# Two weight halves, one tile's statistics on another engine, and Newton steps tile by tile, in a sliding-attention plus gated-MLP kernel

## The chip, the cores and the metric

The kernel runs on one core of a Trainium2 chip. The metric is the device time of one execution in microseconds (us). The core has five engines that run side by side, each taking its own instructions in order: TensorE (PE in the profile, with its weight loads as PEld), VectorE (DVE), ScalarE (ACT), GpSimd (POOL) and SyncE (SP), which here only issues DMA transfers. An engine waits where an instruction needs what another engine or a transfer has not delivered yet.

## The reference

`x` is 2048 tokens by 512 features, in bf16. Both branches read its layernorm `xn`; their outputs are added to `x`.

```python
xn = _layernorm(x, axis=-1)                       # (x - m) / sqrt(v + 1e-5)
# branch A: 32 heads of 16, each token attends to 8 earlier tokens, 2 apart
qkv = xn @ wqkv;  logits = q . k[pos - 2*w] * 16**-0.5;  attn = softmax(logits)
A = (attn-weighted sum of v) @ wo
# branch B: gated MLP with a token-mixing matrix
z  = gelu(xn @ w_in)                              # 2048 x 1376
z1 = z[:, :688];  z2 = _layernorm(z[:, 688:])
g  = w_sp @ z2 + b_sp[:, None]                    # 2048 x 2048 mixing over tokens
B  = (z1 * g) @ w_out
out = x + A + B
```

## The kernel before

The tokens are cut into 16 tiles of 128 rows. The order of the instructions on every engine is written out by hand (`tc.manual_schedule()`): an engine executes what the program issues to it in program order, and semaphores between engines follow from the data. TensorE carries nearly all of the span, in this order: `z2` for tiles 0 to 3, the q and k products, further `z2` tiles between them, head sums (`reduce_heads`), v products, the token mixing (`mix`), the `z1` tiles, and the two output products.

The change is in the first 30 us, which prepare `xn` and start TensorE:

- **Loads.** SP issues, in order, rows of tile 0 and tile 1 (L169, L170), the rows of tiles 2 and 3 together (L171), all 688 columns of the `z2` weights `w_z2` (L172, in the profile `w_z`), then the further rows (`load_x`, L165) and the q and k weights `wqk`. The bias `b_sp` is loaded on ScalarE's queue as 16 rows of 128 (L91), turned by TensorE (L351) and copied by ScalarE into `b_col`.
- **Layernorm of tiles 0 to 3.** `ln_stats(i)` is a `bn_stats` and a `bn_aggr` on VectorE (L185, L186); `roots` is a square root on ScalarE (L194); `recip` a reciprocal on VectorE (L348); `ln_apply` writes the normalised tile `xn` on VectorE (L190); `transpose_pe` turns it in four 128x128 pieces on TensorE (L212) and copies it into `xnT`, on ScalarE for tiles 0 and 1 (L214) and on VectorE for tiles 2 and 3 (L216).
- **Spins.** `spin(n)` issues n small matmuls on a tile of ones (L100) whose results nobody reads; they keep TensorE busy before there is data.
- **`z2` tiles.** One tile is 8 matmuls of 344 columns, 4 slices `kc` of the inner dimension by 2 column halves `hh` (L229), into a pair of PSUM banks (three pairs take turns); ScalarE then applies gelu (L234). Tiles 0 to 3 run as soon as `xnT` has them, and the q and k products of tokens 0 to 511 (`qk_pair`, L272) follow.
- **Layernorm of tiles 4 to 15.** This goes in groups of two tiles. Per group VectorE computes the statistics and three small integer and float steps that give a first guess of 1/sqrt (L200 to L202); GpSimd refines both tiles' guesses by two Newton steps, four small operations each (L204 to L207); VectorE applies, and SP issues a transposing DMA per tile into `xnT` (L219). The loop issues for each round: statistics of group g, guess and Newton steps of group g, then apply and transposes of the group before.

After tile 15's apply VectorE starts `products(0, 0)` and `products(0, 1)` (L301), whose sums `reduce_heads(0, 0)` and `reduce_heads(0, 1)` take on TensorE (L310).

Of the kernel before, what the change touches and what calls it, by code (L numbers as in the profile page):

```python
# [7 lines left out]
BF16 = mybir.dt.bfloat16  # L8
F32 = mybir.dt.float32
ACT = mybir.ActivationFunctionType  # L10
ALU = mybir.AluOpType
PSUM = bass.MemoryType.PSUM

P = 128
S = 2048
D = 512
NT = S // P
C = D // P
H = 32
DH = 16  # L20
DHA = 14
W = 8
DIL = 2
HALO = 16
# [4 lines left out]
F = 1376  # L29
FH = 688  # L30
FHALF = 344
# [10 lines left out]
NEWTON_C = (1.19462228, 1.5 / 1.407904506 ** 2)  # L42
# [3 lines left out]
def kernel(  # L46
# [16 lines left out]
    V = nc.vector  # L63
    A = nc.scalar
    G = nc.gpsimd
    PE = nc.tensor
    SP = nc.sync
# [6 lines left out]
    const = ctx.enter_context(tc.tile_pool(name="const", bufs=1))  # L74
# [7 lines left out]
    ps_aux = pair_b.enter_context(tc.tile_pool(name="ps_aux", bufs=2, space=PSUM))  # L82
    turn = [0]

    def bank_pair(name, two=False):
        turn[0] += 1
        pool = ps_b if turn[0] % 3 == 0 and not two else ps_a
        return pool.tile([P, 2, 512], F32, name=name, tag="mm")

    b16 = const.tile([NT, P], BF16, name="b16")  # L90
    A.dma_start(b16[:], B_b_sp.rearrange("(j p) -> j p", p=P))  # L91


    ones = const.tile([P, P], BF16, name="ones")
    V.memset(ones[:], 1.0)
# [2 lines left out]
    def spin(n):  # L98
        for _ in range(n):
            PE.matmul(idle[:, 0, 0:P], ones[:], ones[:], start=True, stop=True)  # L100

    spin(26)

    ident = const.tile([P, P], BF16, name="ident")
    G.memset(ident[:], 0.0)
# [4 lines left out]
    for c in range(C):  # L110
# [3 lines left out]
                        base=15 - 128 * c, pattern=[[16, 32]], channel_multiplier=-1)  # L114
    mask = const.tile([32, W, HALO], F32, name="mask")
    G.memset(mask[:], 0.0)
    G.affine_select(out=mask[:], in_=mask[:], compare_op=ALU.is_ge, fill=NEG,
                    base=-DIL * (W - 1), pattern=[[DIL, W], [1, HALO]], channel_multiplier=0)
    b_col = const.tile([P, NT], F32, name="b_col")
    stats = const.tile([P, NT, 6], F32, name="stats")  # L120
    mv = const.tile([P, NT, 2], F32, name="mv")
    rstd = const.tile([P, NT], F32, name="rstd")
    hv = const.tile([P, NT], F32, name="hv")
    nt = const.tile([P, NT], F32, name="nt")
    eps_t = const.tile([P, 1], F32, name="eps_t")
# [5 lines left out]
    zrstd = const.tile([P, NT], F32, name="zrstd")  # L131
# [8 lines left out]
    xnT = rpool.tile([P, C, S], BF16, name="xnT")  # L140
# [11 lines left out]
    xnp = early.enter_context(tc.tile_pool(name="xnp", bufs=6))  # L152
    w_z2 = e1.tile([P, C, FH], BF16, name="w_z2")
    wqk = e1.tile([P, C, 2, D], BF16, name="wqk")
    junk = e1.tile([P, FH], BF16, name="junk")


    w_in_r = B_w_in.rearrange("(k p) f -> p k f", p=P)
    wqkv_r = A_wqkv.rearrange("(k p) f -> p k f", p=P)
    xq = []  # L160
# [7 lines left out]
    x0 = xqp.tile([P, 4, D], BF16, name="xq")  # L168
    SP.dma_start(x0[:, 0, :], x2[0:P, :])  # L169
    SP.dma_start(x0[:, 1, :], x2[P:2 * P, :])  # L170
    SP.dma_start(x0[:, 2:4, :], x2[2 * P:4 * P, :].rearrange("(i p) d -> p i d", p=P))  # L171
    SP.dma_start(w_z2[:], w_in_r[:, :, FH:F])  # L172
    xq.append(x0)
    load_x(1)
    for s in range(2):
# [7 lines left out]
    def ln_stats(i):  # L183
        xs = xq[i // 4][:, i % 4, :]
        V.bn_stats(stats[:, i, :], xs)  # L185
        V.bn_aggr(mv[:, i, :], stats[:, i, :])  # L186

    def ln_apply(i):
        xn = xnp.tile([P, D], BF16, name="xn")
        V.tensor_scalar(xn[:], xq[i // 4][:, i % 4, :], mv[:, i, 0:1], rstd[:, i:i + 1], ALU.subtract, ALU.mult)  # L190
        return xn

    def roots(a, b):
        A.activation(rstd[:, a:b], mv[:, a:b, 1], ACT.Sqrt, bias=eps_t[:])  # L194

    def ln_newton(a, b):

        sl = slice(a, b)
        y, h, t = rstd[:, sl], hv[:, sl], nt[:, sl]
        V.tensor_scalar(h, mv[:, sl, 1], EPS, -0.5 / NEWTON_K, ALU.add, ALU.mult)  # L200
        V.tensor_scalar(t.bitcast(I32), h.bitcast(I32), 1, 0x3FFFFFFF, ALU.logical_shift_right, ALU.bitwise_and)
        V.tensor_scalar(y.bitcast(I32), t.bitcast(I32), -1, SEED, ALU.mult, ALU.add)  # L202
        for c in NEWTON_C:
            G.tensor_tensor(t, y, y, ALU.mult)  # L204
            G.tensor_tensor(t, t, h, ALU.mult)
            G.tensor_scalar(t, t, c, None, ALU.add)
            G.tensor_tensor(y, y, t, ALU.mult)  # L207

    def transpose_pe(i, xn):
        pt = ps_aux.tile([P, C, P], BF16, name="pt", tag="aux")  # L210
        for c in range(C):
            PE.transpose(pt[:, c, :], xn[:, c * P:(c + 1) * P], ident[:])  # L212
        if i < 2:
            A.copy(xnT[:, :, i * P:(i + 1) * P], pt[:])  # L214
        else:
            V.tensor_copy(xnT[:, :, i * P:(i + 1) * P], pt[:])  # L216

# [3 lines left out]
    def z2_start(i):  # L221
        pz = bank_pair("pzb")
        for kc in range(C):
            z2_part(i, pz, kc)
        return pz

    def z2_part(i, pz, kc):
        for hh in range(2):
            PE.matmul(pz[:, hh, 0:FHALF], xnT[:, kc, i * P:(i + 1) * P],  # L229
                      w_z2[:, kc, hh * FHALF:(hh + 1) * FHALF],  # L230
                      start=(kc == 0), stop=(kc == C - 1))

    def z2_gelu(i, pz):
        A.activation(z2[:, i, :].rearrange("p (a b) -> p a b", a=2), pz[:, :, 0:FHALF],  # L234
                     ACT.Gelu_apprx_tanh, accum_out=zsum[:, i:i + 1])
# [4 lines left out]
    def z2_tile(i):  # L240
        z2_gelu(i, z2_start(i))
# [13 lines left out]
    def qk_chunk(b, c):  # L255
        tsl = slice(b * 512, (b + 1) * 512)
        pq = bank_pair("pq")
        for s in range(2):
            for kc in range(C):
                PE.matmul(pq[:, s, :], wqk[:, kc, s, c * P:(c + 1) * P], xnT[:, kc, tsl],  # L260
                          start=(kc == 0), stop=(kc == C - 1))
        at = HALO + b % 2 * 512
        A.copy(qk[b // 2][:, :, c, at:at + 512], pq[:])  # L263
# [83 lines left out]
    def recip(i):  # L347
        V.reciprocal(rstd[:, i:i + 1], rstd[:, i:i + 1])  # L348

    pb = ps_aux.tile([P, NT], BF16, name="pb", tag="aux")  # L350
    PE.transpose(pb[:], b16[:], ident[0:NT, 0:NT])  # L351
    spin(9)
    ln_stats(0)
    roots(0, 1)
    A.copy(b_col[:], pb[:])
    ln_stats(1)
    roots(1, 2)
    recip(0)
    transpose_pe(0, ln_apply(0))
    recip(1)  # L360
    spin(4)
    transpose_pe(1, ln_apply(1))
    spin(4)
    ln_stats(2)
    roots(2, 3)
    ln_stats(3)
    roots(3, 4)
    pz0 = z2_start(0)
    z2_gelu(0, pz0)
    recip(2)  # L370
    xn2 = ln_apply(2)
    recip(3)
    xn3 = ln_apply(3)
    pz1 = bank_pair("pzb")
    for kc in range(2):
        z2_part(1, pz1, kc)
    transpose_pe(2, xn2)
    for kc in range(2, C):
        z2_part(1, pz1, kc)
    transpose_pe(3, xn3)  # L380
    z2_gelu(1, pz1)
    z2_tile(2)
    z2_tile(3)


# [2 lines left out]
    for g in groups + (None,):  # L388
        if g:
            for i in range(*g):  # L390
                ln_stats(i)
            ln_newton(*g)
        if prev:
            for i in range(*prev):
                transpose_dma(i, ln_apply(i))
            if prev[0] == 6:
                SP.dma_start(wv[:], wqkv_r[:, :, 2 * D:3 * D])
        prev = g


# [14 lines left out]
    qk_chunk(1, 2)  # L415
    z2_square(5)
    qk_chunk(1, 3)
    for j in range(5):
        load_wsp(j)
        if j == 1:  # L420
            SP.dma_start(w_z1[:], w_in_r[:, :, 0:FH])
# [116 lines left out]
    op = late2.tile([P, DH, NB * TG], BF16, name="op")  # L538
    wo_r = late2.tile([P, DHA, D], BF16, name="wo_r")
    wout = late2.tile([P, MCH, D], BF16, name="wout")  # L540
    G.memset(wout[32:64, MCH - 1, :], 0.0)

    def op_rest(hb, q):

        for k in range(NG):
            for e in range(2):
                q.dma_start(uT[64 + 32 * e:96 + 32 * e, MCH - 1, hb * SB + k * TG:hb * SB + (k + 1) * TG],
                             op[32 * k:32 * k + 32, DHA + e, hb * TG:(hb + 1) * TG])

# [41 lines left out]
    for j in range(3, NT):  # L591
# [6 lines left out]
        if j == 5:  # L598
            SP.dma_start(wout[:, 0:MCH - 1, :], B_w_out[0:(MCH - 1) * P, :].rearrange("(m p) n -> p m n", p=P))
            SP.dma_start(wout[0:FTAIL, MCH - 1, :], B_w_out[(MCH - 1) * P:FH, :])  # L600
            for e in range(2):
                SP.dma_start(wout[64 + 32 * e:96 + 32 * e, MCH - 1, :],
                             A_wo.rearrange("(h d) n -> d h n", d=DH)[DHA + e])
        if 6 <= j < 10:
            k = j - 6
            SP.dma_start(wo_r[32 * k:32 * k + 32, :, :], A_wo.rearrange("(h d) n -> h d n", d=DH)[:, 0:DHA, :])
        if 11 <= j < 13:
# [34 lines left out]
    def out_a(jj, first):  # L642
        for k in range(NG):
            if first:
                pos[jj, k] = ps_o[jj % 2].tile([P, D], F32, name="po")
        for d in range(DHA):
            for k in range(NG):
                PE.matmul(pos[jj, k][:], op[32 * k:32 * k + 32, d, jj * P:(jj + 1) * P],  # L648
                          wo_r[32 * k:32 * k + 32, d, :], start=first and d == 0,
                          stop=(not first or (jj, k) == (3, NG - 1)) and d == DHA - 1, tile_position=(32 * k, 0))  # L650

# [54 lines left out]
```

## Time and profile before

| | |
|---|---|
| time, median of 3 runs | 206.74 us (206.56 to 206.85) |
| the profiled execution: time, span | 206.28 us, 204.6 us |
| TensorE busy | 199.7 us, 98% of the span |
| VectorE, ScalarE, GpSimd busy | 81%, 46%, 8% |
| granted TensorE clock | 1.0 of full speed |
| first `z2` matmul starts | 6.73 us |
| first q/k matmul (`qk_pair`) starts | 11.84 us |
| last apply (tiles 14, 15) starts | 28.68 us |
| `products(0, 0)` and `(0, 1)`, together | 30.49 to 39.24 us |
| first `reduce_heads` matmul | 41.94 us |

The profiled execution is 1.68 us longer than its span: launch and end lie outside of it. Times inside the profile count from the start of the span. The chain of waits is followed back from the last instruction, each step to what released it; a line of it with a queue's name and "q" is the issuing of a transfer. Starts of pipelined instructions can lie a little before the end of the one ahead.

### The profile page before, as it was taken

What the parts mean: (1) busy time and instruction counts of PE and PEld (TensorE: products, weight loads), DVE (VectorE), ACT (ScalarE), POOL (GpSimd) and SP (SyncE); (2) the same over time, 40 slices, a digit from 0 to 9 for tenths busy, and PEclk for the clock granted to TensorE, in tenths of its full rate; (3) what the DMA queues carried; (4) which work ended last, traced back from release to release, by engine and by line L of the source; (5) the groups of instructions that cost most, each with busy time, mean ns of one, the idle gap of its engine ahead of it and who ended that gap; (6) DMA issues with size and microseconds to landing.
All of it is one profiled execution on the core that took longest, in us unless ns stands there. A gap on an engine that the chain in (4) does not pass through costs nothing.

```text
span 204.6 us, 4062 instructions
## 1 busy us (share of the span) xinstructions
PE 199.7 (98%) x1666; PEld 120.1 (59%) x1666; DVE 165.9 (81%) x192; ACT 93.6 (46%) x145; POOL 16.1 (8%) x82
## 2 busy tenths in 40 slices
PE   7999999999999999999999999999999999999994
PEld 6655544555566666656666666666666664444442
DVE  4799949659299499989999999999999988335263
ACT  3868897676879996335733331223333311000000
POOL 5045640000000000100000000000000000000000
PEclk9999999999999999999999999999999999999999
DMA  6974957999000004707857799999756225015633
GB/s 167 365 225 79 187 107 153 187 215 145 0 3 0 3 0 41 170 20 161 125 119 153 176 201 187 196 165 205 141 144 141 56 48 80 10 41 153 240 109 96
DMA packets 67395, 25.64 MB, mean 125 GB/s; under 512 B 57152, under 2 KB 67248, under 8 KB 67248
## 3 DMA queue, kind: packets, MB, share of 16 engines
q1 hardware_dynamic: 66960, 25.24, 58.2%
q8 instruction: 13, 0.21, 0.5%
q10 hardware_dynamic: 416, 0.14, 0.3%
q14 instruction: 6, 0.05, 0.1%
HBM read 9.79 MB, written 2.10 MB: 58 GB/s over the span
## 4 chain that ended last, share of the span: by engine, by line
PE 95%; DMA 2%; SPq 1%; DVE 0%; issue 0%
PE pg L492 37%; PE pq L260 10%; PE po L639 10%; PE pzb L229 9%; PE pz L504 9%; PE pv L285 7%; PE po L648 6%; PE pl L310 4%; PE pq L272 3%; DMA w_z<-in_B_w_in_dram 2%; PE po L621 1%; PE pt L212 0%; SPq L171 0%; DVE ot L623 0%; SPq L170 0%; SPq L169 0%
## 5 line engine op out<-in xcount | busy, mean ns | idle before, releaser
L492 PE MATMUL pg<-z,wspT 128*128 128x344 bf16 x512 | 77.3, 309 | 0.0
L492 PEld LDWEIGHTS <-wspT 128*128 128x128 bf16 x512 | 50.0, 98 | 24.9 <-issue 0.4
L301 DVE TENSOR_TENSOR pr<-qk 128x8192 bf16<-128x8192 bf16 x8 | 35.0, 4424 | 7.4 <-PE pl L310 7.4
L495 ACT ACTIVATE gs<-pg,b_col 128x688 bf16<-128x688 f32 x16 | 13.4, 835 | 52.8 <-PE pg L492 52.8
L558 DVE TENSOR_TENSOR pw<-vp,a_sb 128x4096 bf16<-128x4096 bf16 x16 | 36.2, 2286 | 0.0
L260 PE MATMUL pq<-xnT,wqk 128*128 128x512 bf16 x96 | 21.5, 379 | 0.0
L504 PE MATMUL pz<-w_z,xnT 128*128 128x344 bf16 x128 | 21.3, 309 | 0.0
L229 PE MATMUL pzb<-w_z,xnT 128*128 128x344 bf16 x128 | 20.1, 309 | 0.3 <-DMA w_z<-in_B_w_in_dram 0.3
L639 PE MATMUL po<-wout,uT 128*128 128x512 bf16 x90 | 19.8, 379 | 0.0
L563 DVE TENSOR_TENSOR pw<-pw 128x4096 bf16<-128x4096 bf16 x8 | 18.3, 2289 | 0.1
L655 DVE TENSOR_TENSOR ot<-po,xr 128x512 bf16<-128x512 f32 x15 | 9.7, 687 | 9.4 <-PE po L648 6.9
L229 PEld LDWEIGHTS <-xnT 128*128 128x128 bf16 x128 | 12.3, 98 | 7.2 <-issue 0.7
L504 PEld LDWEIGHTS <-xnT 128*128 128x128 bf16 x128 | 12.4, 98 | 6.5 <-issue 0.4
L260 PEld LDWEIGHTS <-wqk 128*128 128x128 bf16 x96 | 9.3, 98 | 10.9 <-issue 0.4
L639 PEld LDWEIGHTS <-uT 128*128 128x128 bf16 x90 | 8.7, 98 | 10.7 <-issue 0.4
L263 ACT CAST qk<-pq 128x1024 bf16<-128x1024 f32 x12 | 12.2, 1013 | 5.4 <-PE pq L260 5.4
L285 PE MATMUL pv<-xnT,wv 128*32 128x512 bf16 x256 | 14.6, 380 | 0.0
L509 ACT ACTIVATE z<-pz 128x688 bf16<-128x688 f32 x16 | 11.9, 745 | 5.6 <-PE pz L504 5.2
L238 ACT ACTIVATE junk<-z 128x688 bf16<-128x688 bf16 x16 | 12.5, 779 | 0.2
L234 ACT ACTIVATE z<-pzb 128x688 bf16<-128x688 f32 x16 | 11.8, 737 | 1.4 <-PE pzb L229 1.4
L648 PE MATMUL po<-wo_r,op 32*128 32x512 bf16 x224 | 12.3, 374 | 0.0
L285 PEld LDWEIGHTS <-wv 128*32 128x32 bf16 x256 | 9.4, 139 | 4.6 <-issue 0.3
(81 smaller groups left out, 167.5 us busy)
## 6 DMA issues: line engine op xcount, KB each, us to landing
xr<-in_A_x_dram SPq DMA_DIRECT2D x4, 512.0 KB, 4.2
out_dram<-ot SPq DMA_DIRECT2D x15, 128.0 KB, 1.8
wo_r<-in_A_wo_dram SPq DMA_DIRECT2D x4, 448.0 KB, 5.0
w_z<-in_B_w_in_dram SPq DMA_DIRECT2D x2, 688.0 KB, 4.9
xq<-in_A_x_dram SPq DMA_DIRECT2D x2, 512.0 KB, 7.0
wqk<-in_A_wqkv_dram SPq DMA_DIRECT2D x2, 512.0 KB, 7.1
wout<-in_B_w_out_dram SPq DMA_DIRECT2D x1, 640.0 KB, 5.0
a_sb<-in_A_x_dram SPq DMA_DIRECT2D x1, 512.0 KB, 9.2
```

The source lines that it names most:

```text
L229: PE.matmul(pz[:, hh, 0:FHALF], xnT[:, kc, i * P:(i + 1) * P], w_z2[:, kc, hh * FHALF:(hh + 1) * FHALF], start=(kc == 0), stop=(kc == C - 1))
L238: A.activation(junk[:], z2[:, i, :], ACT.Square, accum_out=zsq[:, i:i + 1])
L260: PE.matmul(pq[:, s, :], wqk[:, kc, s, c * P:(c + 1) * P], xnT[:, kc, tsl], start=(kc == 0), stop=(kc == C - 1))
L285: PE.matmul(pv[32 * k:32 * k + 32, dd, :].rearrange("p (b t) -> p b t", b=NB), wv_v[:, kc, 2 * d2 + dd, :], xnT_g[:, kc, :, k, :], start=( ...
L301: V.tensor_tensor(pr[:], qk[hb][:, 0, :, HALO:HALO + SB].unsqueeze(1).broadcast_to([P, 2, C, SB]), shifted(qk[hb][:, 1, :, off:off + SB]), ...
L492: PE.matmul(pg[:, hh, 0:FHALF], wsps[j][:, k, :], z2[:, k, hh * FHALF:(hh + 1) * FHALF], start=(k == 0), stop=(k == NT - 1))
L495: A.activation(gs[:], pg[:, :, 0:FHALF], ACT.Identity, bias=b_col[:, j:j + 1])
L504: PE.matmul(pz[:, hh, 0:FHALF], xnT[:, kc, j * P:(j + 1) * P], w_z1[:, kc, hh * FHALF:(hh + 1) * FHALF], start=(kc == 0), stop=(kc == C - 1))
L558: V.tensor_tensor(pw[:], shifted(vp[:, :, hb, off:off + P]), a_sb[:, 2 * p:2 * p + 2, osl].unsqueeze(2).broadcast_to([P, 2, DH, P]), ALU.mult)
L563: V.tensor_tensor(pws[p - 1][:], pws[p - 1][:], pw[:], ALU.add)
L639: PE.matmul(pos[jj, k][:], uT[:, m, i * P:(i + 1) * P], wout[:, m, :], start=first and m == 0, stop=not first and m == MCH - 1)
L648: PE.matmul(pos[jj, k][:], op[32 * k:32 * k + 32, d, jj * P:(jj + 1) * P], wo_r[32 * k:32 * k + 32, d, :], start=first and d == 0, stop=(n ...
```

## The change

The first rows are unchanged, but `w_z2` is loaded in two transfers, columns 0 to 343 ahead of the rows of tiles 2 and 3 and columns 344 to 687 behind them. Tiles 0 and 1 take the first column half first: the order on TensorE is transposes 0, spin(7), transposes 1, then (tile 0, half 0), (tile 1, half 0), (tile 0, half 1), transposes 2, (tile 1, half 1), half of tile 2, transposes 3, the rest of tile 2, tile 3. The copies of `xnT` on ScalarE are cut in two.

Tile 1's mean and variance come from ScalarE: an Identity with a running sum, a Square with a running sum, and a square root. A first square root on a constant stands ahead of everything on ScalarE. Tile 4's `bn_stats` goes in two halves into the start-up of tiles 2 and 3.

The Newton steps run per tile in two fused operations instead of four, so a group still has eight, each one column wide with one or two of its scalars read per partition from memory. In the loop, the guess and the Newton steps of group g now come behind apply and transposes of the group before.

The bias is loaded by a transposing DMA on SP's queue after tile 15's transposes, and copied by GpSimd. The 26 + 9 spins become one run of 35.

```diff
-    b16 = const.tile([NT, P], BF16, name="b16")
-    A.dma_start(b16[:], B_b_sp.rearrange("(j p) -> j p", p=P))
-    spin(26)
+    spin(35)
...
     SP.dma_start(x0[:, 1, :], x2[P:2 * P, :])
+    SP.dma_start(w_z2[:, :, 0:FHALF], w_in_r[:, :, FH:FH + FHALF])
     SP.dma_start(x0[:, 2:4, :], x2[2 * P:4 * P, :].rearrange("(i p) d -> p i d", p=P))
-    SP.dma_start(w_z2[:], w_in_r[:, :, FH:F])
+    SP.dma_start(w_z2[:, :, FHALF:FH], w_in_r[:, :, FH + FHALF:F])
...
-        for c in NEWTON_C:
-            G.tensor_tensor(t, y, y, ALU.mult)
-            G.tensor_tensor(t, t, h, ALU.mult)
-            G.tensor_scalar(t, t, c, None, ALU.add)
-            G.tensor_tensor(y, y, t, ALU.mult)
+        for i in range(a, b):
+            y, h, t = rstd[:, i:i + 1], hv[:, i:i + 1], nt[:, i:i + 1]
+            for c in NEWTON_C:
+                G.tensor_scalar(t, y, y, h, ALU.mult, ALU.mult)
+                G.tensor_scalar(y, t, c, y, ALU.add, ALU.mult)
...
         if i < 2:
-            A.copy(xnT[:, :, i * P:(i + 1) * P], pt[:])
+            for c in range(0, C, 2):
+                A.copy(xnT[:, c:c + 2, i * P:(i + 1) * P], pt[:, c:c + 2, :])
...
+    def z2_half(i, pz, hh):
+        for kc in range(C):
+            z2_part(i, pz, kc, (hh,))
...
-    pb = ps_aux.tile([P, NT], BF16, name="pb", tag="aux")
-    PE.transpose(pb[:], b16[:], ident[0:NT, 0:NT])
-    spin(9)
+    A.activation(zrstd[:, 0:1], eps_t[:], ACT.Sqrt)
     ln_stats(0)
+    A.activation(junk[:, 0:D], x0[:, 1, :], ACT.Identity, scale=-1.0 / D, accum_out=mv[:, 1, 0:1])
     roots(0, 1)
-    A.copy(b_col[:], pb[:])
-    ln_stats(1)
-    roots(1, 2)
+    A.activation(junk[:, 0:D], x0[:, 1, :], ACT.Square, bias=mv[:, 1, 0:1], accum_out=mv[:, 1, 1:2])
+    A.activation(rstd[:, 1:2], mv[:, 1, 1:2], ACT.Sqrt, bias=eps_t[:], scale=1.0 / D)
     recip(0)
     transpose_pe(0, ln_apply(0))
+    spin(7)
     recip(1)
-    spin(4)
-    transpose_pe(1, ln_apply(1))
-    spin(4)
+    xn1 = xnp.tile([P, D], BF16, name="xn")
+    V.tensor_scalar(xn1[:], x0[:, 1, :], mv[:, 1, 0:1], rstd[:, 1:2], ALU.add, ALU.mult)
+    transpose_pe(1, xn1)
     ln_stats(2)
     roots(2, 3)
     ln_stats(3)
     roots(3, 4)
-    pz0 = z2_start(0)
+    pz0 = bank_pair("pzb")
+    pz1 = bank_pair("pzb")
+    z2_half(0, pz0, 0)
+    z2_half(1, pz1, 0)
+    z2_half(0, pz0, 1)
     z2_gelu(0, pz0)
     recip(2)
     xn2 = ln_apply(2)
     recip(3)
+    transpose_pe(2, xn2)
+    z2_half(1, pz1, 1)
+    z2_gelu(1, pz1)
     xn3 = ln_apply(3)
-    pz1 = bank_pair("pzb")
-    for kc in range(2):
-        z2_part(1, pz1, kc)
-    transpose_pe(2, xn2)
-    for kc in range(2, C):
-        z2_part(1, pz1, kc)
+    pz2 = bank_pair("pzb")
+    z2_part(2, pz2, 0)
+    z2_part(2, pz2, 1)
+    V.bn_stats(stats4[:, 0, :], xq[1][:, 0, 0:D // 2])
     transpose_pe(3, xn3)
-    z2_gelu(1, pz1)
-    z2_tile(2)
+    V.bn_stats(stats4[:, 1, :], xq[1][:, 0, D // 2:D])
+    V.bn_aggr(mv[:, 4, :], stats4[:])
+    z2_part(2, pz2, 2)
+    z2_part(2, pz2, 3)
+    z2_gelu(2, pz2)
     z2_tile(3)
...
         if g:
             for i in range(*g):
-                ln_stats(i)
-            ln_newton(*g)
+                if i > 4:
+                    ln_stats(i)
         if prev:
             for i in range(*prev):
                 transpose_dma(i, ln_apply(i))
...
+        if g:
+            ln_newton(*g)
         prev = g
...
     qk_chunk(1, 3)
+    SP.dma_start_transpose(b_t[:], B_b_sp.rearrange("(j p) -> j p", p=P))
+    G.tensor_copy(b_col[:], b_t[:])
```

More of the change, by code (lines that the diff above doesn't have):

```diff
@@ L21 @@
 DHA = 14
+ZV = (7, 8, 13, 14, 15)
 W = 8
@@ L119 @@
     b_col = const.tile([P, NT], F32, name="b_col")
+    b_t = const.tile([P, NT], BF16, name="b_t")
+    stats4 = const.tile([P, 2, 6], F32, name="stats4")
     stats = const.tile([P, NT, 6], F32, name="stats")
@@ L225, in z2_start, with z2_part @@
         return pz
-    def z2_part(i, pz, kc):
-        for hh in range(2):
+    def z2_half(i, pz, hh):
+        for kc in range(C):
+            z2_part(i, pz, kc, (hh,))
+    def z2_part(i, pz, kc, halves=(0, 1)):
+        for hh in halves:
             PE.matmul(pz[:, hh, 0:FHALF], xnT[:, kc, i * P:(i + 1) * P],
```

## The prediction

> **What bounds the kernel now.** I read the page's chain of waits first, then the same chain for the first 13 us, then the timeline of ScalarE, VectorE and GpSimd up to 45 us.
>
> ```profile
> PE 95%; DMA 2%; SPq 1%; DVE 0%; issue 0%
> ...
> 2.19 4.50 DMA w_z<-in_B_w_in_dram
> 6.69 0.04 issue
> 6.73 1.91 PE pzb L229 x12
> ```
>
> From 6.73 us on TensorE is the chain, without a gap, to the last 3 us. So only two things can count: when that stream starts, and whether the change opens a gap in it. The weights hold the start only just: by TensorE's timeline the weight load for the first `z2` matmul was at 6.35 us, and the wait for `w_z` was 0.31 us. Nothing else on TensorE moves, so the head cannot bring more than a few tenths.
>
> The rows of ScalarE and VectorE that feed tiles 0 and 1:
>
> ```profile
> 3.75 0.18 DVE L186 BATCH_NORM_AGGREGATE mv<-stats 128x2 f32<-128x6 f32 x1
> ...
> 4.64 0.13 DVE L348 RECIPROCAL rstd<-rstd 128x1 f32<-128x1 f32 x1
> 4.81 0.41 DVE L190 TENSOR_SCALAR xn<-xq,mv,rstd 128x512 bf16<-128x512 bf16 x1
> 5.13 0.16 DVE L348 RECIPROCAL rstd<-rstd 128x1 f32<-128x1 f32 x1
> ...
> 7.27 0.13 DVE L348 RECIPROCAL rstd<-rstd 128x1 f32<-128x1 f32 x1
> ```
>
> And one round of the later tiles: GpSimd's first steps of the group of tiles 6 and 7, VectorE's apply of tiles 4 and 5 beside them, the last apply, and the products behind it.
>
> ```profile
> 14.65 0.19 POOL L204 TENSOR_TENSOR nt<-rstd 128x2 f32<-128x2 f32 x1
> 14.92 0.20 POOL L205 TENSOR_TENSOR nt<-nt,hv 128x2 f32<-128x2 f32 x1
> ...
> 14.66 0.73 DVE L190 TENSOR_SCALAR xn<-xq,mv,rstd 128x512 bf16<-128x512 bf16 x2
> ...
> 28.68 0.73 DVE L190 TENSOR_SCALAR xn<-a_sb,mv,rstd 128x512 bf16<-128x512 bf16 x2 [1.79 <-POOL rstd L207]
> 30.40 0.18 DVE L424 COPY qk<-qk 128x64 bf16<-128x64 bf16 x1 [0.99 <-ACT qk L263]
> 30.49 8.75 DVE L301 TENSOR_TENSOR pr<-qk 128x8192 bf16<-128x8192 bf16 x2
> ```
>
> Today VectorE sets the pace of these rounds (applies at 14.66, 17.53, 20.39: 2.87 us each), and GpSimd's eight steps (about 0.28 us from start to start, 2.25 together) hide beside the next statistics. The products end at 39.24; the second `reduce_heads`, which needs them, starts 0.92 us (16 of 32 matmuls in 1.84) after 42.01, at 42.93. That cover of 3.7 us is what the change uses up.
>
> **The head, step by step.** Tile 1's rows land at 1.26 + 2.3 = 3.56 us (issue and landing of L170). Identity over 512 from SBUF: the Square over 688 takes 0.78; the 1024 cast against the 512 copy gives (1.013 - 0.587) / 512 = 0.83 ns an element, so 0.78 - 0.15 = 0.63 us. Its accumulator read starts 0.10 before its end and lasts 0.20, as at L238: mean at 4.31. Tile 0's root is queued behind it, at 4.22 instead of 3.96, ends 4.52; reciprocal 4.59 instead of 4.64, because VectorE has lost tile 1's statistics. So tile 0 gains 0.05 only. The Square reads a bias, which is worth 0.09 (L495 0.835 against L509 0.745): from 4.43, sum at 5.25; root 5.29 to 5.59; tile 1's reciprocal at 5.66, against 5.13 now.
>
> From that reciprocal to the transposes of tile 1 is 0.66 us (5.13 to 5.79), and 0.24 more to what follows on TensorE (6.03). The transposes of tile 1 stand ahead of the first half of `z2`, so TensorE starts at 6.56: 0.17 gained on 6.73. The first 344 columns do not hold it: tiles 2 and 3's 256 KB, issued at the same 1.72, landed 2.9 us later, so 344 KB land by about 5.3.
>
> But VectorE now runs 0.53 late. Reciprocal 1 to reciprocal 2 is 2.14 as before, to the transposes 0.66: tile 2's transposes start at 8.46. TensorE, with 12 matmuls at 0.146, is there at 8.35: 0.1 wait. Transposes 0.40, copy 0.43, three hops of about 0.035: tile 2 usable at 9.36, TensorE there at 9.26: 0.1. The same for tile 3: 10.84 against 10.74: 0.1. Eight matmuls later the q/k products start at 12.01, against 11.84. **Head: +0.17 us**, the gain eaten by three waits. Bounds: if ScalarE's chain were as quick as VectorE's (reciprocal 1 at 5.13), 6.1 us from there (2.80 to tile 2's transposes, then 20 matmuls and two transposes, 3.3) gives 11.2, -0.6; a chain 0.2 slower gives +0.4.
>
> The second half of `w_z2` is needed at 7.75. All of it landed at 6.69; the bytes ahead of it are the same, but its rows are 688 bytes, so 512 packets more. At the present 63 ns of a packet (60% of 5 us on 16 engines for 764) over 16 engines that is at most 2.0 us, at the least 0. I take 0.4, near the bytes: landing 7.1, no wait; the upper end gives 0.9.
> [...] No run here shows 688-byte rows yet.
>
> The dummy root, the split copies and tile 4's early statistics go into idle stretches. The gelu table load (1.28) moves to 8.2, gelu of tile 0 to 9.5, needed by tile 3's matmuls at 10.8. The bias leaves TensorE and ScalarE and puts one transposing DMA on SP, some 1.2 us by L219, ahead of the `w_sp` loads, which are first used at 73 us: nothing. GpSimd's copy waits for that DMA; only memsets of `z1` stand behind it.
>
> **The rounds.** Behind the change the guess for the next group waits in VectorE's queue behind the second apply, which waits for GpSimd's eighth step. So the chain closes on itself: one round is 8 steps plus about 1.0 us (0.03 to the apply, 0.33 to the next slot, three guesses of 0.21 less overlap 0.58, 0.08 to GpSimd). With g from step to step, the first group starts at 12.8, tile 15's step ends at 12.8 + 48 g + 5.0, the two products end 0.5 + 8.75 later: 27.1 + 48 g. TensorE needs them at 42.93 + 0.15 = 43.1. **The cover is gone at g = 0.333; beyond, each 10 ns costs 0.48 us.**
>
> What is g? The trace shows no GpSimd operation with scalars read from memory. Lower end: L204 to L207 as they are, 0.28. An immediate tensor_scalar, L206, steps at 0.30. Upper end by other engines' pointers: on ScalarE 0.09 each; on VectorE, L252 against L190 (0.459 for 688, 0.411 for 512) leave 0.27 fixed where L244 has 0.163, 0.054 for each of two. New operations have two and one pointers, 1.5 on average: 0.30 + 0.135 = 0.435. GpSimd's own second stream operand costs nothing (L205 0.213 with two, L206 0.217 with one). I take half of VectorE's price, 0.027 each: **g = 0.34**, between these two rows. That is 48 x 0.007 = 0.35 us at the products, and 0.1 to 0.2 at the q/k products of tokens 512 to 1023, which need tile 7: its transpose would land at 22.5 (second round's step end 19.2 + apply 0.45, + landing 2.6 with some 0.2 of queue), against 22.25 + 0.15.
> [...]
>
> **Sum.** Head +0.17, rounds +0.35 and +0.15, rest 0: +0.7 us. On the profiled execution 206.28 + 0.7 = 207.0; its 206.28 lies 0.46 under the median, to which I add the same: **207.4**.
>
> **Rivals.** (a) *GpSimd's pointers are nearly free*, g up to 0.33: the rounds grow to 3.4 to 3.65 us but stay under the 3.7 us cover; only the head remains, 206.9, no change. For it: L205 against L206. Against it: both other engines pay. (b) *Faster*: ScalarE's sums come early and tile 2 is not late; reciprocal 1 before 5.3 and g under 0.33, time 206.1 to 206.4. It needs 0.35 us off a chain whose every row is measured on other shapes. (c) *GpSimd pays in full*, g 0.37 to 0.43: tile 6, tile 11 and tile 15 come late too; products alone give +1.8 to +4.7, time 208.7 to 211.6. (d) The second weight half lands late, up to +0.9 at the head: 0.05, inside the others' ranges.
>
> **Numbers.** Forecast (g 0.333 to 0.37) 0.33; (a) with (d) 0.29; (b) 0.13; (c) 0.25. Range 206.2 to 210.5 leaves out half of (c) and part of (b). 0.2%, 0.4 us, is about what a measurement of this kernel can tell from no change. Faster 0.13, same 0.29, slower 0.58.
>
> **What would show it.** Right: the first `z2` matmul near 6.55 and q/k near 12.0; VectorE idle before the reciprocal of tile 1, released by ScalarE; GpSimd steps near 0.34; the second apply of each round waiting for GpSimd; products starting near 34.5, and TensorE waiting before its second head sum. Wrong: GpSimd steps at or below 0.30 with products before 33; q/k starting before 11.6; or a TensorE wait on the second weight half.

## The result: 2.6 us slower, nearly all of it in the closed loop of GpSimd and VectorE

| | before | changed |
|---|---|---|
| median | 206.68 us | 209.31 us (209.05 to 209.59, 4 runs) |
| ratio to before | | 1.0131 (95%: 1.0118 to 1.0145) |
| profiled execution: time, span | 206.28, 204.6 us | 209.53, 207.8 us |
| first `z2` matmul, first q/k matmul | 6.73, 11.84 us | 6.62, 12.71 us |
| GpSimd's work for two tiles, first start to last end | 2.2 us | 3.0 us |
| one round of two tiles | 2.87 us | 4.03 us |
| `products(0, 0)` and `(0, 1)` end | 39.24 us | 46.08 us |

The profiled executions lie 0.40 under the median of before and 0.22 over the median of the changed kernel, so their difference, 3.25 us, overstates the change by 0.62. Medians and ratios here leave out the few executions that ran at a lower granted clock (one of the six of run e4 below: 355.67 us at 0.56).

The page's chain of waits, changed kernel. TensorE had 95% of it before:

```profile
PE 77%; DVE 9%; POOL 7%; issue 2%; DMA 2%; SPq 1%
```

Most of the first 46 us of the chain has moved to other engines. The timelines of VectorE and GpSimd for the third round (start, duration, engine and line, operation, what ended the idle time before it):

```profile
21.33 0.17 DVE L203 TENSOR_SCALAR rstd<-nt 128x2 int32<-128x2 int32 x1
...
24.64 0.41 DVE L191 TENSOR_SCALAR xn<-xq,mv,rstd 128x512 bf16<-128x512 bf16 x1 [1.06 <-POOL rstd L208]
24.96 0.16 DVE L201 TENSOR_SCALAR hv<-mv 128x2 f32<-128x2 f32 x1
...
25.36 0.17 DVE L203 TENSOR_SCALAR rstd<-nt 128x2 int32<-128x2 int32 x1
...
36.90 0.41 DVE L191 TENSOR_SCALAR xn<-a_sb,mv,rstd 128x512 bf16<-128x512 bf16 x1 [1.06 <-POOL rstd L208]
```

```profile
21.60 0.34 POOL L207 TENSOR_SCALAR nt<-rstd,hv 128x1 f32<-128x1 f32 x1 [1.03 <-DVE rstd L203]
22.04 0.26 POOL L208 TENSOR_SCALAR rstd<-nt,rstd 128x1 f32<-128x1 f32 x1
...
24.33 0.26 POOL L208 TENSOR_SCALAR rstd<-nt,rstd 128x1 f32<-128x1 f32 x1
25.63 0.34 POOL L207 TENSOR_SCALAR nt<-rstd,hv 128x1 f32<-128x1 f32 x1 [1.03 <-DVE rstd L203]
```

Read them as one circle. VectorE's guess ends at 21.50, GpSimd works from 21.60 to 24.59, the second apply waits 1.06 us for it and starts at 24.64, the next guess stands behind that apply and ends at 25.53, and GpSimd, idle for 1.03 us, starts at 25.63. Each engine waits once for the other: 4.03 us a round. What this costs is in the timeline of TensorE, first before, then changed:

```profile
22.25 7.07 PE L260 MATMUL pq<-xnT,wqk 128*128 128x512 bf16 x32
...
30.32 7.07 PE L260 MATMUL pq<-xnT,wqk 128*128 128x512 bf16 x32
...
41.94 1.91 PE L310 MATMUL pl<-pr,rsel 128*32 128x512 bf16 x32
43.68 3.63 PE L285 MATMUL pv<-xnT,wv 128*32 128x512 bf16 x64
```

```profile
23.49 7.08 PE L266 MATMUL pq<-xnT,wqk 128*128 128x512 bf16 x32
...
31.95 7.07 PE L266 MATMUL pq<-xnT,wqk 128*128 128x512 bf16 x32 [0.21 <-DMA xnT<-xn]
...
43.57 1.05 PE L316 MATMUL pl<-pr,rsel 128*32 128x512 bf16 x16
46.12 1.05 PE L316 MATMUL pl<-pr,rsel 128*32 128x512 bf16 x16 [1.51 <-DVE pr L307]
```

The lines are the q/k products of tokens 512 to 1023, those of tokens 1024 to 1535 and the head sums; the v products behind the sums start at 43.68 before and at 46.98 now. The lag of the changed kernel is 0.87 us after the head, then 1.24, 1.63, 1.63 and, behind the second head sum, 3.30. From there to the end it stays: 1.67 of it is the wait for the products, 0.76 the transposes of tiles 6, 7 and 11 landing late.

These parts are not separate prices. From the second head sum to the end of the span both profiles take 161.7 us (204.6 - 42.93 and 207.8 - 46.12), and in the changed kernel that sum starts 0.04 us after the products end. So the end of the products alone sets the time there: without the earlier waits TensorE would have waited longer at this place. The products end 6.84 us later than before; 1.1 of that is the later first step of GpSimd (13.54 against 12.44), the rest the longer rounds, and 3.7 was cover.

The head, in VectorE's timeline:

```profile
5.41 0.16 DVE L354 RECIPROCAL rstd<-rstd 128x1 f32<-128x1 f32 x1 [0.42 <-ACT rstd L362]
5.61 0.41 DVE L368 TENSOR_SCALAR xn<-xq,mv,rstd 128x512 bf16<-128x512 bf16 x1
6.86 0.69 DVE L186 BATCH_NORM_STATS2 stats<-xq 128x6 f32<-128x512 bf16 x1 [0.84 <-DMA xq<-in_A_x_dram]
```

Tile 1's reciprocal waits for ScalarE, as expected, but then comes a wait that the prediction did not have: the rows of tiles 2 and 3, now queued behind the first weight half, land at 2.19 + 4.65 = 6.84 us.

### The profile page after: what moved, and what is told of

It reads as the page before. It is cut to its first block, busy times and chain, and to the rows that moved or that the text cites. A ratio compares the mean times of both kernels' runs of the same rounds, so it can differ in the third digit from the quotient of the medians.

```text
span 207.8 us, 4069 instructions
## 1 busy us (share of the span) xinstructions
PE 201.6 (97%) x1664; PEld 120.6 (58%) x1664; DVE 165.7 (80%) x191; ACT 95.0 (46%) x151; POOL 21.2 (10%) x83
## 4 chain that ended last, share of the span: by engine, by line
PE 77%; DVE 9%; POOL 7%; issue 2%; DMA 2%; SPq 1%
PE pg L511 36%; PE po L658 9%; PE pz L523 9%; PE pv L291 7%; PE po L667 6%; PE pzb L235 5%; DVE pr L307 4%; POOL nt L207 4%; POOL rstd L208 3%; PE pl L316 3%; DMA xq<-in_A_x_dram 2%; PE pq L266 2%; DVE xn L191 1%; DVE stats L186 1%; PE po L640 1%
## 5 line engine op out<-in xcount | busy, mean ns | idle before, releaser
L235 PE MATMUL pzb<-w_z,xnT 128*128 128x344 bf16 x128 | 20.7, 310 | 0.0
```

## The experiments

### Which part costs it: operations and place, apart and together

The GpSimd part has two edits: the operations (four for two tiles at once, against two fused ones per tile) and the place (ahead of the apply of the group before, or behind it). Three kernels undo one or both in the changed kernel, a fourth puts both into the kernel before. All four ran on one chip.

```diff
 # e1: both undone.  e2: place undone.  e3: operations undone.
-            for c in NEWTON_C:
-                G.tensor_scalar(t, y, y, h, ALU.mult, ALU.mult)
-                G.tensor_scalar(y, t, c, y, ALU.add, ALU.mult)
+        for c in NEWTON_C:                       # e1, e3
+            G.tensor_tensor(t, y, y, ALU.mult)
...
+            ln_newton(*g)                        # e1, e2: ahead of transpose_dma(i, ln_apply(i))
         if prev:
...
-        if g:
-            ln_newton(*g)
```

Both undone:

> The changed kernel with the whole GpSimd part put back: the four unfused operations for two tiles at once, issued ahead of the apply of the group before. My theory has two separate losses, the head (q/k start 0.87 us later, because VectorE waits for the rows of tiles 2 and 3 behind the first weight half) and the closed loop of GpSimd and VectorE (2.4 us). It expects the head alone: q/k at about 12.7 us, no wait of TensorE behind it, rounds of 2.9 us, time 207.1 to 207.6. Rival 1, all of the loss is the loop: 206.7. Rival 2, the head costs most: 208.5 or more.

Only the place undone:

> The changed kernel with the fused per-tile operations kept, but the guess and the Newton steps issued ahead of the apply of the group before, as in the kernel before. My theory: GpSimd's 3.0 us of a group then set the rounds by themselves (3.0 us instead of 4.03), tile 15's apply at 31.5 to 32, products end near 41, before TensorE needs them (43.8), so the time is that of the kernel with the whole GpSimd part put back, 207.1 to 207.6. Rival, the dearer operations are the loss wherever they stand: 209.0 to 209.3.

Only the operations undone:

> The changed kernel with the four unfused operations for two tiles at once, kept at the new place behind the apply. My theory: a round is 2.25 + 1.03 = 3.3 us, tile 15's apply near 32.3, products end near 41.5, TensorE needs them at 43.8: no wait, 207.1 to 207.6. Rival, the place alone is the loss: 209.0 to 209.3.

Nothing but the GpSimd part, in the kernel before:

> The kernel before with nothing but the GpSimd part of the change: fused per-tile operations behind the apply. My theory: first step at 12.4 us, rounds of 4.03, second apply of the last round at 35.7, products end at 44.9 where TensorE needs them at 42.93: 2.0 us lost, 208.7 (208.4 to 208.9). Rival, the loop only hurts because the head is already late: at most 207.2.

| kernel | median, us | ratio to before (95%) |
|---|---|---|
| before, same runs | 206.59 | |
| both undone (e1) | 206.64 | 0.9998 (0.9981 to 1.0016) |
| place undone, fused operations (e2) | 207.03 | 1.002 (1.0001 to 1.004) |
| operations undone, new place (e3) | 206.97 | 1.0012 (0.9995 to 1.0029) |
| before with both (e4) | 208.57 | 1.0096 (1.0062 to 1.013) |

Either edit alone costs 0.4 us (the intervals reach 0.8 and 0.6); both together cost 2.0, in a kernel whose head is untouched. So place and price act together, as the closed loop has it. VectorE's timeline for the last rounds shows how: with the fused operations at the old place,

```profile
28.67 0.43 DVE L191 TENSOR_SCALAR xn<-a_sb,mv,rstd 128x512 bf16<-128x512 bf16 x1 [0.17 <-POOL rstd L208]
...
31.64 0.41 DVE L191 TENSOR_SCALAR xn<-a_sb,mv,rstd 128x512 bf16<-128x512 bf16 x1 [1.06 <-POOL rstd L208]
32.06 8.76 DVE L307 TENSOR_TENSOR pr<-qk 128x8192 bf16<-128x8192 bf16 x2
```

and with the unfused operations at the new place:

```profile
29.39 0.74 DVE L191 TENSOR_SCALAR xn<-a_sb,mv,rstd 128x512 bf16<-128x512 bf16 x2 [0.68 <-POOL rstd L208]
32.89 0.74 DVE L191 TENSOR_SCALAR xn<-a_sb,mv,rstd 128x512 bf16<-128x512 bf16 x2 [2.28 <-POOL rstd L208]
33.62 8.76 DVE L307 TENSOR_TENSOR pr<-qk 128x8192 bf16<-128x8192 bf16 x2
```

Rounds of 3.13 us (19.28, 22.40, 25.54, 28.67) and of 3.50 end the products at 40.8 and 42.4. TensorE starts the head sums at 42.60 and 42.77 there and needs the second product 0.87 later: covered both times. What is left is 0.24 and 0.31 us between the first later `z2` tile and the q/k products behind it, waits for the transposes of tiles 6 and 7.

The first run also corrects my reading of the head. I expected 0.4 to 0.9 us from it, by the 0.87 between the two profiles, and rival 1 (206.7) held; e2 and e3 ended 0.1 under their ranges for the same reason. Its profile has q/k at 12.30, and the repeat of e4 below, whose head is that of the kernel before, has 12.61, because its weights landed 5.3 us after their issue instead of 4.5 and its first `z2` matmul started at 7.49 instead of 6.73. The landing of the first loads differs from execution to execution, by 0.8 us in these two and by 0.4 for the rows of tiles 2 and 3 in the changed head (4.6 us after their issue in the changed kernel, 4.2 in e1 and e2). One profile of each can't price the head.

### Where in the kernel before: the trace of the GpSimd part alone

> The kernel before with nothing but the GpSimd part of the change, once more for a trace at full clock. Theory: rounds of 4.03, last apply at 35.7, TensorE waits 1.5 to 2 us before the second head sum, 208.4 to 208.9.

Measured 209.27 against 206.71 on another chip, 1.0122 (1.0099 to 1.0144), 0.4 us above what I expected. The waits are those of the changed kernel, on VectorE and on TensorE:

```profile
36.74 0.41 DVE L190 TENSOR_SCALAR xn<-a_sb,mv,rstd 128x512 bf16<-128x512 bf16 x1 [1.07 <-POOL rstd L207]
37.15 13.09 DVE L301 TENSOR_TENSOR pr<-qk 128x8192 bf16<-128x8192 bf16 x3
```

```profile
45.96 1.05 PE L310 MATMUL pl<-pr,rsel 128*32 128x512 bf16 x16 [1.52 <-DVE pr L301]
```

The last apply is one microsecond later than the 35.7 expected: the weights landed 0.8 us later than in the profile I had counted from, and VectorE's copies of tiles 2 and 3, ahead of the loop in its queue, wait for TensorE (1.7 us in all, 0.9 in the kernel before). The two runs put the GpSimd part at 2.0 and 2.6 us.

### What one scalar from memory costs

```diff
-                G.tensor_scalar(t, y, y, h, ALU.mult, ALU.mult)
+                G.tensor_scalar(t, y, y, 0.5, ALU.mult, ALU.mult)
```

> The changed kernel with the variance term of the first fused operation (L207) given as an immediate, so it reads one scalar from memory instead of two; every row then uses the same variance in the Newton steps. If each scalar read from memory costs about 0.06 us (0.217 with none, 0.271 with one, 0.341 with two in the profiles so far): L207 at 0.27 to 0.28, a group 0.25 us shorter, rounds of 3.77, last apply 1.5 us earlier near 35.4, and the 1.5 us wait before the second head sum gone: 207.2 to 207.8. Rival, the fused form costs what it does because of its two arithmetic steps, not its operands: L207 stays at 0.34 and the time at 209.1 to 209.5.

The kernel leaves the row's variance out of the Newton steps and so does not compute the layernorm; only its time and its trace are used.

Measured 207.19 us, ratio to before 1.0021 (0.9997 to 1.0044): 2.1 us came back for one operand. Rounds are 3.73 us, the last apply starts at 34.75 instead of 36.90, TensorE waits no more for the transposes of tiles 6, 7 and 11, and 0.3 us are left before the second head sum:

```profile
43.97 1.05 PE L316 MATMUL pl<-pr,rsel 128*32 128x512 bf16 x16 [0.31 <-DVE pr L307]
```

The groups of GpSimd in this kernel,

```profile
L208 POOL TENSOR_SCALAR rstd<-nt,rstd 128x1 f32<-128x1 f32 x24 | 6.4, 265 | 2.6
L207 POOL TENSOR_SCALAR nt<-rstd 128x1 f32<-128x1 f32 x24 | 6.3, 261 | 15.7 <-DVE rstd L203 14.6
```

in the changed kernel (mean ns of one behind the bar's first comma),

```profile
L207 POOL TENSOR_SCALAR nt<-rstd,hv 128x1 f32<-128x1 f32 x24 | 8.2, 341 | 16.0 <-DVE rstd L203 14.8
L208 POOL TENSOR_SCALAR rstd<-nt,rstd 128x1 f32<-128x1 f32 x24 | 6.5, 271 | 2.4
```

and the one with an immediate alone in the kernel before:

```profile
L206 POOL TENSOR_SCALAR nt<-nt 128x2 f32<-128x2 f32 x12 | 2.6, 217 | 1.1
```

The operation with the same arithmetic falls from 341 to 261 ns when it reads one scalar less, so the second scalar costs 80 ns. L206 is 44 to 54 ns below the operations with one scalar, but it also has one arithmetic step instead of two, on two columns instead of one; what the first scalar costs by itself no run here shows. The rival, that the fused arithmetic is what is dear and that the time stays at 209.1 to 209.5, falls.

### The head

Four kernels with the GpSimd part undone or kept, and the rows of tiles 2 and 3 moved ahead of the first weight half:

```diff
+    SP.dma_start(x0[:, 2:4, :], x2[2 * P:4 * P, :].rearrange("(i p) d -> p i d", p=P))
     SP.dma_start(w_z2[:, :, 0:FHALF], w_in_r[:, :, FH:FH + FHALF])
-    SP.dma_start(x0[:, 2:4, :], x2[2 * P:4 * P, :].rearrange("(i p) d -> p i d", p=P))
```

GpSimd part undone:

> The changed kernel with the whole GpSimd part put back, and the rows of tiles 2 and 3 loaded ahead of the first weight half instead of behind it. Theory: the rows land near 4.7 instead of 6.4, VectorE does not wait for them, q/k start at 11.7 instead of 12.3: 0.5 us faster than with the rows behind, 206.0 to 206.3. Rival, the first half then lands too late for its first matmul (after 6.6) and nothing is gained: 206.5 to 206.8.

> The run with rows first and the GpSimd part put back, once more to narrow its interval against the kernel before. Theory: the head starts q/k 0.1 us and the first matmul 0.45 us earlier than the kernel before: 206.1 to 206.4, 0.1 to 0.25% faster. Rival: no difference.

First 206.20 against 206.64 (0.9976, 0.9949 to 1.0004), with q/k at 11.75 and VectorE not waiting for the rows; then 206.57 against 206.71 (0.9999, 0.9986 to 1.0012), with q/k at 12.26, because tile 1's rows took 2.6 us instead of 2.1 to land there. No gain over the kernel before is shown.

The statistics of tile 1 back on VectorE, with the rows first and with the rows behind:

```diff
-    A.activation(junk[:, 0:D], x0[:, 1, :], ACT.Identity, scale=-1.0 / D, accum_out=mv[:, 1, 0:1])
     roots(0, 1)
-    A.activation(junk[:, 0:D], x0[:, 1, :], ACT.Square, bias=mv[:, 1, 0:1], accum_out=mv[:, 1, 1:2])
-    A.activation(rstd[:, 1:2], mv[:, 1, 1:2], ACT.Sqrt, bias=eps_t[:], scale=1.0 / D)
+    ln_stats(1)
+    roots(1, 2)
...
-    transpose_pe(1, xn1)
+    transpose_pe(1, ln_apply(1))
```

> As the run with the rows first, and tile 1's statistics back on VectorE (bn_stats, bn_aggr, one square root). Theory: reciprocal of tile 1 at 5.1 as in the kernel before instead of 5.34, tile 2 0.2 earlier, the first matmul bound by the first weight half: 205.9 to 206.2. Rival, statistics on ScalarE are the better half of the head: 206.3 or more.

> The changed kernel with the whole GpSimd part put back and tile 1's statistics back on VectorE, the rows of tiles 2 and 3 still behind the first weight half. Theory: VectorE waits for those rows until 6.4 either way, so the place of tile 1's statistics does not show: 206.5 to 206.8, q/k at 12.2 to 12.4. Rival, ScalarE's longer chain is what delays the head: 206.2 or less.

Measured 206.84 (0.9995, 0.997 to 1.0019) and 206.98 (1.0011, 0.999 to 1.0033). The second missed its range by 0.2 us, but VectorE waited for the rows until 6.53, as expected; in its profile 0.23 us more than in e1 pass between the first later `z2` tile and the q/k products behind it (19.28 to 23.01, in e1 19.21 to 22.71). The first missed by more, and its rival's bound (206.3 or more) held: VectorE had tile 2 ready 0.26 us earlier, yet q/k started at 11.80, as with ScalarE's statistics, since the second weight half, landed at 7.6, held the third group of four matmuls, as its chain of waits shows:

```profile
2.70 4.89 DMA w_z<-in_B_w_in_dram
7.59 0.04 issue
7.63 0.74 PE pzb L235 x4
```

In this profile an earlier VectorE moves nothing. Why its runs spread from 206.2 to 207.5 is open; the kernel before spread from 206.2 to 208.4 beside them.

Rows first, with the loop kept, and with the fused operations at the old place:

> The changed kernel with nothing but the load order altered: rows of tiles 2 and 3 ahead of the first weight half. Theory, head and loop are separate terms: q/k at 11.8, GpSimd's first step 0.7 us earlier (12.8), six rounds of 4.03 as before, products end near 45.2 and TensorE needs them at 42.7: about 2.5 us lost on the run with rows first and the GpSimd part put back (206.2), 208.5 to 208.9. Rival, the early rows feed the loop so much earlier that it hides: under 207.5.

> Rows first, and GpSimd's fused per-tile operations at the old place, ahead of the apply. Theory: the fused form is dearer (3.0 us of a group against 2.25) and sets rounds of 3.1, so tiles 6 and 7 come 0.2 to 0.4 us late as in the run with the fused form at the old place: 206.3 to 206.7, slower than with the unfused form. Rival, tile 4 and 5 come earlier and that helps: 206.1 or less.

Measured 208.94 (1.0107, 1.0087 to 1.0126) and 207.02 (1.0012, 1.0 to 1.0024). The early rows bring q/k to 11.88, yet TensorE still waits 1.54 us before the second head sum: its own earlier start gains nothing. What can gain is the loop: VectorE's statistics behind its first guess start at 12.52 instead of 13.35, the second head sum starts at 45.45 instead of 46.12, and the ratio is 1.0107 against the changed kernel's 1.0131, though the intervals overlap. The fused operations at the old place do not help; their run is 0.3 us above the range. Its profile can't put that on GpSimd alone: the stretch from the first later `z2` tile to the q/k products, where TensorE's weight load waits 0.5 us for a transpose, is 0.3 us longer than in e1 (19.26 to 23.07, 3.81 against 3.50), and in the head the second weight half landed near 8.1 (5.4 us after its issue at 2.7), the third group of four matmuls started at 8.19 and q/k at 12.35.

## Why the prediction came out as it did

The sign, the place and the mechanism were right; the size was 0.7 us against a measured 2.63, and the case that came true was rival (c), to which I gave 0.25. That the time lies in the range is owed to its width: it spans 4.3 us and takes in half of (c).

- **The loop.** Its build was right: a round is GpSimd's work plus about 1.0 us (measured 4.03 - 3.0), the cover before the second head sum is 3.7 us. The term that was mis-sized is g. I took 0.027 us for each scalar read from memory, half of VectorE's price, and got 0.34; measured are 80 ns for the second and eight steps in 3.0 us, 0.375 in the mean. Put into the prediction's own line, 27.1 + 48 x 0.375 = 45.1 against 43.1 gives 2.0 us where 0.35 stood, and the GpSimd part alone measured 2.0 and 2.6. ScalarE's 0.09 us was the nearer row; going down from it and from VectorE's 0.054 because a second stream operand showed no cost on GpSimd (0.213 us with two, 0.217 with one) was the mistake.
- **The sum.** It adds the head, the q/k products and the products of the head sums, although the last of these contains the others. By its own figures the products end at 27.1 + 48 x 0.34 = 43.4, which puts the second head sum 0.5 us behind the 42.93 of before, in all and not beside 0.17 and 0.15.
- **The q/k products of tokens 512 to 1023**: 0.15 forecast for tile 7, 0.37 measured at tiles 6 and 7, and 0.39 more at tile 11. Both are gone in e5, where g is smaller.
- **The head.** Forecast +0.17, measured nothing that can be told from 0, nor from the forecast (e1: 0.9998, 0.9981 to 1.0016). The steps were off in both directions. ScalarE's chain was 0.25 quicker (reciprocal of tile 1 at 5.41 against 5.66): 0.12 of it because it started earlier (3.44 against 3.56), the rest in shorter hops between the instructions. The prediction asked when the first and the second weight half land, and forgot the rows of tiles 2 and 3 between them: they landed at 6.84 in the changed kernel, and VectorE waited 0.84 us for them.
- **The weight halves.** The first landed at 6.1, against 5.3 forecast, and did not hold TensorE. The second took 5.2 us from its issue and landed near 7.9, against 7.1 forecast. TensorE's ninth `z2` matmul, the first to need it, starts 0.26 us after the eighth (7.74, 8.00), where one takes 0.15: some 0.1 us, which lies inside TensorE's later wait for tile 2. What makes it land late no run here isolates. From 1.7 to 6.8 us the changed kernel moved 260 GB/s and the kernel before 293, but the whole weights, issued at the same 2.19, took 4.5 us in the kernel before and 5.3 in the repeat of e4, so a landing moves by 0.8 us without the halves. That the 688-byte rows cost anything, or that they cost nothing, is not shown; the 0.4 us in the prediction was my estimate.
- **The bias, tile 4's early statistics**: no wait of TensorE shows either, as forecast. ScalarE's copies, now split, show only in its weight loads, which wait 0.4 us for them in all; TensorE then waits 0.38 us for VectorE's tile 2 in any case.

## What to carry to other kernels

When a producer's next input stands in its consumer's queue behind the instruction that waits for it, the two engines take turns, and the round is the sum of both (here 3.0 and 1.0 us, 4.03 a round; 3.13 with the same operations at the old place): look for it whenever work is moved behind an apply or a store. Price a fused operation also by what it reads, not only by the steps it saves; here eight operations for two tiles replaced eight, each with one or two scalars to read, and took 0.8 us longer (3.0 against 2.2), 0.3 of it for the second scalar (four times 80 ns). A cover that a trace shows (3.7 us here) is spent by all later edits together: either of these two fitted under it alone. And waits on the way to one late result are not added up: the last one contains them.

## What the runs showed of the hardware

- A fused [128, 1] operation on GpSimd takes 261 to 274 ns with one scalar read from memory and 341 to 344 with two (changed kernel, e5, the repeat of e4); one with an immediate, a single arithmetic step and two columns takes 217. Dependent ones start about 0.1 us after the end of the one before.
- One of these, at 27.56 us, took 0.43 us instead of 0.26 in the round where VectorE's apply (27.45 to 27.86) lay over its start. In the kernel before, the first steps at 17.70, 20.57, 23.43 and 26.31, all inside an apply, took 0.29 to 0.31 instead of 0.19, but the second step at 14.92, also inside an apply, took 0.20. Whether the apply is what made the others longer no run tests.
- The spins stayed slow longer in the changed kernel's profile, 35 matmuls of 128 columns in 3.91 us (0.11 each), while before the last 9 took 0.68 together, with a granted clock of 1.00 shown in both. In e2, with the same head, the last 10 took 0.76, in e1 1.27, so this differs between executions. It did not set the end of the head, where VectorE's rows came later.
